# k of batch 0's second and last third on 96 and 112 partitions, where it was on 94 and 100, in a windowed-attention and ReGLU kernel

## The chip, the cores and the metric

The kernel runs on one core of a Trainium2 chip. The core has five engines with a program each: TensorE (PE, matmuls; its weight loads are shown apart as PEld), VectorE (DVE), ScalarE (ACT), GpSimd (POOL) and SyncE (SP, which here only issues transfers). They work in parallel, each in the order of its own program, and wait for each other by semaphores. 16 DMA engines move data between the memory of the device and SBUF, the core's memory of 128 partitions. The metric is the device time of one execution in microseconds (us), the median of three runs; lower is better. The profile is of one further execution, and its span is a little shorter than the device time.

## The reference

Attention for 4 batches of 8 heads, 768 positions and head size 64, in which a query sees the first 4 positions ("sinks") and the last 128; then a ReGLU feed-forward (FFN) over all 3072 tokens.

```python
scores = scale * np.matmul(q, k.transpose(0, 1, 3, 2))
keep = is_sink | in_window          # pos < 4, or 0 <= i - j < 128
scores = np.where(keep, scores, -1000000000.0)
scores = scores - np.max(scores, axis=-1, keepdims=True)
a = np.exp(scores)
a = a / (np.sum(a, axis=-1, keepdims=True) + 1e-09)
attn = np.matmul(a, v)
x = attn.transpose(0, 2, 1, 3).reshape(3072, 512)
out = (np.maximum(x @ w_gate, 0) * (x @ w_val)) @ w_out   # d_ff 1536
```

All inputs and the output are float32.

## The kernel before

**Units.** The attention is cut into units of one head pair (two heads, 128 rows of head dimension together). The first batch is cut into thirds along the positions, so that the FFN can begin after a third: kinds A (positions 0 to 251), B (252 to 499) and C (500 to 767), four units each (A0 to A3, B0 to B3, C0 to C3), in this order. Batches 1 to 3 have four units each of kind F (all 768 positions). The table `GEO` (line 22) holds each kind's geometry. Its entry `k=(r0, pp, nn)` says how k is loaded: from row r0 on, on pp partitions with nn consecutive rows each, pp times nn rows in all. B and C need some rows ahead of their first query, for the window: B the keys 124 to 499, C 372 to 767.

**Steps of a unit.** `load_kq` (line 136) issues two transfers for k, one for each head, then two for q; a partition's nn rows are contiguous in device memory, 1 KB for nn = 4. They land in float32 staging tiles: `kf`, `qf` for A, C and F, and for B in `stage`, which borrows the memory of a later tile (line 435). `cast` (line 157) makes bfloat16 of them on POOL (`kn`, `qn`, `vn`). `T` (line 178) transposes k and q on PE, nn transposes for k, and copies them out of PSUM: ACT writes `kT` (line 191), DVE and ACT one half of `qz` each (line 200), and for each key block that has the sinks ACT a copy of 124 of its columns into `kTs` (line 213). `S` (line 226) is scores, exp on ACT (line 236) and mask on DVE (line 238). `V` (line 240) multiplies by v, in which a block of ones also gives the row sums; `norm0` (line 368) divides on DVE and writes `xT`, the input of the FFN, for batch 0 without a way through memory.

Which rows of k stand in which transpose follows from pp and nn, and so do the column of `kTs`' source, `p0 = (124 * j + 4 - self.kr) // kn_` (line 212), and the size of the copy at line 191. Nothing else in the code knows the partition count.

**FFN.** `chunk(b, c0, n, m)` (line 387) does one block of 128 hidden columns of n tokens: four matmuls with `wg` (line 392), relu on ACT, four with `wv` (line 398), product on DVE. `ffn2` (line 404) does the second matmul with `wo` (line 411) and stores the result. Chunks of 0 to 11 belong to A's tokens, 12 to 23 to B's, and so on. A chunk of the first block waits for `xT` of all four A units. `load_w(c)` loads columns for chunks 3c to 3c+2 of each block, with a conversion to bfloat16 during the transfer; it is issued from POOL.

**Order.** All is written out by hand in program order; there is no planner. SP's queue first issues A's loads, then those of the four B units, for each k, q and v (lines 436 to 438), then C's; a load for a later unit waits until the buffer it writes is free. The A units are done one after the other, with the casts and transposes of B0 and B1 between them. Weight loads are calls in this order too: `load_w(0)` behind the casts of A2, `load_w(1)` behind the casts of B0, `load_w(2)` behind those of B1, `load_w(3)` behind those of k and q of B2. Since POOL issues them in its own program order, a cast that waits for its data holds back the weight load behind it.

Then stages of attention (`unit_stages`, line 500) are put between the chunks by the function `want` (line 557): chunk ci is preceded by so many stages, in the first block 1.5 on average, and a B unit has three: S; T of the next unit with the casts of the one after it; V of the unit before it. The transposes of B1 stand ahead of chunk 0, those of B2 ahead of chunk 2, those of B3 ahead of chunk 4, in PE's program.

Of the kernel before, what the change touches and what calls it, by code (L numbers as in the profile page):

```python
# [21 lines left out]
GEO = {  # L22
    "A": dict(q0=0, n=252, q=(0, 128, 2), k=(0, 128, 2), js=(0, 1), sink=(1,),
              groups=[[(0, 0, 255), (1, 128, 128)]], parts=[(0, 256, [(0, 0, 255), (1, 128, 128)])]),
    "B": dict(q0=252, n=248, q=(252, 128, 2), k=(124, 94, 4), js=(1, 2, 3), sink=(2,),
              groups=[[(1, 252, 127), (2, 252, 248), (3, 376, 132)]],
              parts=[(252, 256, [(1, 252, 127), (2, 252, 248), (3, 376, 132)])]),
    "C": dict(q0=500, n=268, q=(480, 96, 3), k=(368, 100, 4), js=(3, 4, 5, 6), sink=(4, 6),
              groups=[[(3, 480, 147), (4, 500, 248)], [(5, 624, 144), (6, 748, 20)]],
              parts=[(480, 288, [(3, 480, 147), (4, 500, 248), (5, 624, 144), (6, 748, 20)])]),  # L30
    "F": dict(q0=0, n=768, q=(0, 128, 6), k=(0, 128, 6), js=(0, 1, 2, 3, 4, 5, 6), sink=(1, 3, 5),
# [589 lines left out]
```

The softmax here doesn't subtract the row's maximum and nothing guards it: scores larger than these inputs give would overflow.

## Time and profile before

| what | value |
|---|---|
| device time, median of 3 | 329.45 us (328.45 to 330.43) |
| span of the profiled execution | 326.9 us |
| PE busy | 263.6 us (81%), 1868 matmuls |
| DVE, ACT, POOL busy | 164.7, 163.4, 95.4 us |
| chain that ended last | PE 52% of the span |
| DMA | 33.64 MB, mean 103 GB/s |
| loads of k for B | 8 issues of 94 KB, from SP |
| loads of k for C | 8 issues of 100 KB, from SP |

Busy shares are means over the span; the page's second part cuts the span into 40 slices of 8.2 us, one digit each, in tenths. A row of the timeline has start, duration, engine, line, operation, output <- input, shape and count, and in brackets the idle time ahead of it on its engine, with what ended that. "SPq" is SP's queue: the duration is that of issuing, not of the transfer. The list of waits has the sum in us, how often, and the longest. In a table of windows each engine has its busy time and its count of instructions; the last three columns are the granted PE clock (1.00 is full), the busy share of the 16 DMA engines (it can pass 1 where packets of two queues overlap on an engine) and the rate in GB/s.

### The profile page before, as it was taken

To read this page: it belongs to the slowest core of one execution; us is meant where nothing else is said; L and a number is where in the kernel's file an instruction comes from. 1 tells how busy PE (TensorE), PEld (TensorE's weight loads), DVE (VectorE), ACT (ScalarE), POOL (GpSimd) and SP (SyncE) were. 2 spreads that over 40 slices of the span, in tenths; PEclk is the share of its full clock that TensorE was granted. 3 is DMA by queue.
4 is the path that set the end of the run, shared out by engine and by line. 5 is a ranking of instruction groups with operands and counts; after the bars stand their busy time and mean duration, and the time that the engine had idled before them with its cause. 6 is when DMAs were issued, how large, how long until landed. Compare 5 with 4: busy or idle time off the path is not lost.

```text
span 326.9 us, 5251 instructions
## 1 busy us (share of the span) xinstructions
PE 263.6 (81%) x1868; PEld 171.3 (52%) x1868; DVE 164.7 (50%) x340; ACT 163.4 (50%) x300; POOL 95.4 (29%) x159
## 2 busy tenths in 40 slices
PE   2443355665668888775999999999999999999995
PEld 1222244553447776553666666666666555555552
DVE  4467141764777557754364746565553542332220
ACT  5643233564457887453556566565764333333321
POOL 7626215454456555705040505042000000000000
PEclk9999875987989999999899999999999999999999
DMA  4769894948569868839192845253422120111002
GB/s 130 123 122 170 126 167 118 191 87 146 117 131 109 162 106 141 173 84 170 53 185 73 166 115 91 81 61 88 55 66 65 36 80 35 41 50 40 32 32 96
DMA packets 55313, 33.64 MB, mean 103 GB/s; under 512 B 34268, under 2 KB 51436, under 8 KB 55288
## 3 DMA queue, kind: packets, MB, share of 16 engines
q1 hardware_dynamic: 25096, 25.48, 27.1%
q0 software_dynamic: 29104, 7.57, 24.0%
q10 hardware_dynamic: 1088, 0.26, 0.4%
q8 instruction: 14, 0.23, 0.3%
q14 instruction: 11, 0.09, 0.1%
HBM read 34.43 MB, written 6.44 MB: 125 GB/s over the span
## 4 chain that ended last, share of the span: by engine, by line
PE 52%; ACT 0%; issue 0%; ACTq 0%
PE op L411 17%; PE vp L398 14%; PE gp L392 14%; PE ops L248 3%; PE sps L232 2%; PE tq L195 1%; PE tk L188 1%; ACT ot L415 0%; ACTq L415 0%
## 5 line engine op out<-in xcount | busy, mean ns | idle before, releaser
L400 DVE TENSOR_TENSOR hT<-gs,vp 128x384 bf16<-128x384 f32 (+3 forms) x108 | 54.6, 506 | 73.0 <-PE vp L398 59.4
L398 PE MATMUL vp<-xT,wv 128*128 128x384 bf16 (+3 forms) x432 | 83.6, 318 | 4.0 <-ACT gs L395 2.1
L392 PE MATMUL gp<-xT,wg 128*128 128x384 bf16 (+3 forms) x432 | 83.8, 318 | 3.8 <-DVE xT L364 3.8
L411 PE MATMUL op<-wo,hT 128*128 128x512 bf16 x288 | 79.0, 383 | 0.0
L395 ACT ACTIVATE gs<-gp 128x384 f32<-128x384 f32 (+3 forms) x108 | 49.2, 456 | 40.3 <-PE gp L392 39.6
L398 PEld LDWEIGHTS <-wv 128*128 128x128 bf16 x432 | 43.7, 101 | 30.1 <-issue 8.5
L236 ACT ACTIVATE ee<-sps 128x1006 bf16<-128x1006 f32 (+6 forms) x52 | 47.1, 906 | 15.9 <-PE sps L232 15.4
L238 DVE TENSOR_TENSOR ee<-ee,msk 128x1006 bf16<-128x1006 bf16 (+6 forms) x52 | 37.2, 715 | 33.5 <-ACT ee L236 33.5
L392 PEld LDWEIGHTS <-wg 128*128 128x128 bf16 x432 | 40.8, 101 | 19.4 <-issue 0.2
L151 POOL DMA_DIRECT2D vn<-in_v_dram x32 | 26.2, 824 | 73.6 <-PE ops L248 69.5
L411 PEld LDWEIGHTS <-hT 128*128 128x128 bf16 x288 | 28.4, 99 | 23.0 <-issue 0.6
L188 PE MATMUL tk<-ident,kn 128*128 128x128 bf16 (+2 forms) x112 | 11.7, 244 | 33.7 <-POOL kn L163 33.2
L248 PE MATMUL ops<-ee,vn 128*128 128x248 bf16 (+9 forms) x264 | 29.1, 253 | 8.9 <-ACT qz L200 5.1
L232 PE MATMUL sps<-qz,kT 128*128 128x251 bf16 (+6 forms) x136 | 28.8, 266 | 5.2 <-ACT kT L191 1.9
L248 PEld LDWEIGHTS <-vn 128*128 128x128 bf16 x264 | 23.4, 105 | 18.0 <-issue 8.7
L191 ACT COPY kT<-tk 128x768 bf16<-128x768 bf16 (+3 forms) x24 | 14.9, 622 | 32.5 <-PE tk L188 32.4
L364 DVE TENSOR_TENSOR xT<-oab,R 64x768 bf16<-64x768 f32 x24 | 24.2, 1007 | 10.1 <-DMA R<-rcp_tmp 10.0
L252 ACT COPY oab<-ops 65x752 f32<-65x752 f32 (+1 forms) x24 | 19.1, 795 | 20.1 <-PE ops L248 20.0
L188 PEld LDWEIGHTS <-kn 128*128 128x128 bf16 (+2 forms) x112 | 8.4, 110 | 39.5 <-POOL kn L163 36.2
L200 DVE COPY qz<-tq 64x768 bf16<-64x768 bf16 (+2 forms) x24 | 16.5, 686 | 20.9 <-PE tq L195 20.8
L232 PE MATMUL sps<-qz,kTs 128*128 128x248 bf16 (+3 forms) x104 | 25.9, 272 | 0.0
L200 ACT COPY qz<-tq 64x768 bf16<-64x768 bf16 (+2 forms) x24 | 14.1, 585 | 22.9 <-DVE qz L200 21.6
(61 smaller groups left out, 188.6 us busy)
## 6 DMA issues: line engine op xcount, KB each, us to landing
out_dram<-ot SPq DMA_DIRECT2D x24, 256.0 KB
kf<-in_k_dram SPq DMA_DIRECT2D x24, 192.0 KB
qf<-in_q_dram SPq DMA_DIRECT2D x24, 192.0 KB
R<-rcp_tmp SPq DMA_DIRECT2D x12, 384.0 KB
vn<-in_v_dram POOLq DMA_DIRECT2D x24, 96.0 KB, 3.4
wg<-in_moe_w_gate_dram POOLq DMA_DIRECT2D x4, 384.0 KB, 8.6
wv<-in_moe_w_val_dram POOLq DMA_DIRECT2D x4, 384.0 KB, 11.4
wo<-in_moe_w_out_dram POOLq DMA_DIRECT2D x3, 512.0 KB, 7.9
```

Of the source, the lines that this page charges most:

```text
L151: eng.dma_start(out=dst[:, o + j0:o + j0 + nj, h, 0:64], in_=bass.AP(src.tensor, src.offset + 124 * j0 * D, [[D, 128], [124 * D, nj], [1, ...
L200: (nc.scalar.copy if h else nc.vector.tensor_copy)(qz[s][r, h, z0:z0 + qp * qn_].rearrange("d (p n) -> d p n", n=qn_), pq[r, 0:qp * qn_].r ...
L232: nc.tensor.matmul(out=ps[:, h, c:c + w], lhsT=self.kw(j), rhs=qz[s][:, h, self.zo + qa:self.zo + qa + w], start=True, stop=True)
L236: nc.scalar.activation(x, ps[:, :, 0:c], Act.Exp, bias=0.0, scale=scale)
L238: nc.vector.tensor_tensor(x, x, bc(msk[:, m0:m0 + c], 2), op=Alu.mult)
L248: nc.tensor.matmul(out=ps[:, h, qa - q0:qa - q0 + w], lhsT=vn[s][:, self.vo + j, h, :], rhs=ee[s][:, gi, h, c:c + w], start=i == 0, stop=i ...
L364: nc.vector.tensor_tensor(xTs[b][64 * h:64 * h + 64, p, :], oab[0:64, h, :], R[:, h, :], op=Alu.mult)
L392: nc.tensor.matmul(out=gp[:, 0:n], lhsT=wg[:, ko, m * 128:(m + 1) * 128], rhs=x[:, ko, c0:c0 + n], start=ko == 0, stop=ko == KO - 1)
L395: nc.scalar.activation(gs[:, 0:n], gp[:, 0:n], Act.Relu, bias=0.0, scale=1.0)
L398: nc.tensor.matmul(out=vp[:, 0:n], lhsT=wv[:, ko, m * 128:(m + 1) * 128], rhs=x[:, ko, c0:c0 + n], start=ko == 0, stop=ko == KO - 1)
L400: nc.vector.tensor_tensor(hT[:, m, c0:c0 + n], gs[:, 0:n], vp[:, 0:n], op=Alu.mult)
L411: nc.tensor.matmul(out=op, lhsT=hTs[b][:, m, t * 128:(t + 1) * 128], rhs=wo[:, m, :], start=m == 0, stop=m == FM - 1)
```

## The change

Two entries of the table change. B's k is loaded from row 116 on 96 partitions with 4 rows each (384 rows, up to row 499 as before), where it was row 124 on 94 partitions (376 rows); C's from row 320 on 112 partitions (448 rows), where it was row 368 on 100 (400 rows). The eight and 48 rows more lie ahead of what is needed, and are read and transposed for nothing. It is for the way in which a transfer is spread over the DMA engines, which goes by the number of partitions.

```diff
-    "B": dict(q0=252, n=248, q=(252, 128, 2), k=(124, 94, 4), js=(1, 2, 3), sink=(2,),
+    "B": dict(q0=252, n=248, q=(252, 128, 2), k=(116, 96, 4), js=(1, 2, 3), sink=(2,),
...
-    "C": dict(q0=500, n=268, q=(480, 96, 3), k=(368, 100, 4), js=(3, 4, 5, 6), sink=(4, 6),
+    "C": dict(q0=500, n=268, q=(480, 96, 3), k=(320, 112, 4), js=(3, 4, 5, 6), sink=(4, 6),
```

No instruction is added, removed or moved on any engine. For eight units the transposes of k get 96 and 112 columns for 94 and 100, ACT's copies at line 191 384 and 448 columns for 376 and 400, POOL's casts of k two and twelve partitions more, and the transfers are wider accordingly. The start columns of the `kTs` copies move with r0, and their widths stay.

## The prediction

> **What bounds the kernel now.** I began with the page's 40 slices (8.2 us each): where is TensorE (PE) not full?
>
> ```profile
> PE   2443355665668888775999999999999999999995
> DMA  4769894948569868839192845253422120111002
> ```
>
> Full from slice 20 on: whatever is saved ahead of that only counts if the late part starts earlier. The first seven slices (to 57 us) are at 20 to 50%. So next the waits, with the window 14 to 54 us:
>
> ```profile
> POOL kn L163 <- DMA stage<-in_k_dram: 22.1, 4, 8.6
> PEld L188 <- POOL kn L163: 18.8, 4, 6.3
> PE tk L188 <- POOL kn L163: 17.5, 4, 6.1
> ACT kT L191 <- PE tk L188: 17.0, 4, 6.2
> ```
>
> This is one chain, seen on four engines: GpSimd (POOL) waits four times, 22.1 us in all, for k of the second third (kind B); its cast frees PE's transposes, these ScalarE's (ACT) copy. Nothing overtakes: PE runs in program order, the FFN chunks behind the transposes. The timeline of POOL gives the dates:
>
> ```profile
> 20.07 0.61 POOL L163 CAST kn<-stage 94x512 bf16<-94x512 f32 x1 [5.76 <-DMA stage<-in_k_dram]
> 28.54 2.23 POOL L163 CAST kn<-stage 94x512 bf16<-94x512 f32 x1 [2.44 <-DMA stage<-in_k_dram]
> 38.65 0.61 POOL L163 CAST kn<-stage 94x512 bf16<-94x512 f32 x1 [5.30 <-DMA stage<-in_k_dram]
> 50.81 0.61 POOL L163 CAST kn<-stage 94x512 bf16<-94x512 f32 x1 [8.59 <-DMA stage<-in_k_dram]
> ```
>
> and that of PE what stands behind them (chunks 0, 2 and 4 are the L392 rows that follow each transpose):
>
> ```profile
> 30.83 0.49 PE L188 MATMUL tk<-ident,kn 94*128 94x94 bf16 x4 [4.42 <-POOL kn L163]
> 31.36 1.05 PE L392 MATMUL gp<-xT,wg 128*128 128x252 bf16 x4
> ...
> 39.32 0.50 PE L188 MATMUL tk<-ident,kn 94*128 94x94 bf16 x4 [4.24 <-POOL kn L163]
> ...
> 51.48 0.50 PE L188 MATMUL tk<-ident,kn 94*128 94x94 bf16 x4 [6.06 <-POOL kn L163]
> ...
> 53.03 1.05 PE L392 MATMUL gp<-xT,wg 128*128 128x252 bf16 x4
> ```
>
> Why is k late? Is the DMA full? Two windows, one while only B's loads run (weights landed), one under a weight load; the last columns are granted clock, DMA share, GB/s:
>
> ```profile
> 20.00:23.00 3.00, 1.42 (x11) 1.10 (x12) 1.58 (x4) 0.47 (x1) 1.00 (x2) 1.00 0.17 27
> 15.00:19.00 4.00, 1.53 (x9) 0.88 (x7) 3.25 (x8) 2.93 (x6) 0.00 (x0) 1.00 1.26 216
> ```
>
> POOL waits through both. In the first the 16 engines are busy to 0.17, which is 2.7 engines, and move 27 GB/s; in the second 216 GB/s, 13.5 per engine. 27/13.5 = 2 engines. B's loads crawl over about two engines while fourteen lie idle. The issuing queue feels it too: two k loads take 0.72 us to issue at 10.7 us, but
>
> ```profile
> 31.95 5.06 SPq L142 DMA_DIRECT2D stage<-in_k_dram  x2
> 37.05 5.83 SPq L142 DMA_DIRECT2D stage<-in_q_dram  x2
> ```
>
> **What the skill says.** (1) The Trainium skill, "DMA: Bandwidth & Descriptors", section "Why a DMA increments its semaphore by 16 and not by 1": a DMA runs on the largest k up to 16 that divides the slowest dimension of both sides; it names 128 or 96 partitions as 16 and 100 as 10. By that rule 94 = 2 x 47 gives 2, 112 gives 16. The trace agrees for 94 (2.0 engines above); for 100 it shows nothing separately. (2) Same page, "Issuing engines are not separate DMA queues": loads from SyncE and from GpSimd share the same 16 engines. The trace agrees: k lands slowest where weights run beside it (8.6 us of waiting). (3) "TensorE: Matmul & The Clock Gate", Part 1: an idle stretch of about 3.4 us halves PE's clock. Agrees: 0.50 granted at 39 to 42 us, after the gap from 35.1 to 39.3.
>
> **The change, part by part.**
>
> *B's k on 16 engines.* A pair of k loads (two heads, 94 rows of 1 KB each) puts 94 KB on each of two engines; now 192 rows on 16, 12 KB each. Engine 0 also carries 8 KB of q and 12 KB of v per unit (128-partition tiles, evenly shared), so per unit 114 KB become 32, for four units 456 become 128 KB. At the 13.5 GB/s of a loaded engine: 34 us become 9.5. The old span, first issue 10.7 to last cast 50.8, is 40 us, so this accounts for it. k, q, v of each unit queue in this order, so q and v come early too.
>
> *What then holds the first third.* I walk the old timelines without the k waits. B0's k would be there at about 14.5, when POOL has done A's last piece (14.3). T of B0 then follows S of A3 on PE at 17.9 and not 20.7. VectorE (DVE) is the next limit: its mask of A3 ends at 21.1 in any case; then qz, which came at 22.50, at 21.1, so ACT's qz, kTs and output copies are 1.4 us earlier. DVE's chain of two normalisations, 24.33 to 28.42, starts at 22.9 and ends at 27.0. That gives xT of A3, for which chunk 0 waits; T of B1 no longer does (needed at 24.6, k there by 18 to 20). Chunk 0: 27.0, not 31.36. Saved 4.4.
>
> *Chunks 0 to 4.* Unhindered pace: chunk 4 starts at 53.03, chunk 9 at 66.47 (same timeline), 13.44/5 = 2.7 us, with transposes, scores, sums and copies of one unit per two chunks included. Chunk 4 thus starts at 27.0 + 4 x 2.7 = 37.8, not 53.03: 15.2 saved.
>
> *Do the weights hold it up?* POOL issues them between the casts: now at 10.7, 24.6, 31.9, 40.7. Without k waits at about 11, 17, 20.5, 24. One pair is 0.79 MB as written; four, with four B units (2.1 MB), make 5.2 MB, at 215 GB/s 24 us: all landed at about 36 to 38. Chunk 3 (36) needs the second pair, chunk 6 (43) the third, chunk 9 (51) the fourth. Hidden, with little to spare; B3's k is wanted at 37 too.
>
> *After 54 us.* I take the rest to move as a block: POOL's waits there are for PE and for its own v loads, the units go one by one, and PE is full from 150 us on.
>
> *Added work.* Wider transposes (280 ns for 94x94 and 227 for 100x100 in different clocks, so width is lost in them); ACT's kT copies: 472 ns for 376 columns, 492 for 400, 0.8 ns a column: 4 x 8 + 4 x 48 columns = 0.2 us, at most. More bytes: 4 x 4 + 4 x 24 KB = 112 KB, 0.5 us of the full DMA, spread. Casts have the same length per partition (610 and 604 ns for 94 and 100): nothing. All of it lies beside the new slack.
>
> *C's k on 16 engines.* 100 KB on ten engines becomes 112 on 16. Only one wait of 0.7 us is put down to it: at most 0.7, which I leave out, since C's loads are issued early.
>
> Sum: 329.45 - 15.2 = **314.2 us**. Unknown costs: landing under a saturated DMA (k for B3 0 to 3 us late), pace (1.8 to 2.9 us between single chunks in the trace, 2.2 to 2.9 as a mean): saving 12 to 17.
>
> **Rivals.**
> 1. *DMA as a whole takes over.* All weights now go out within 15 us on top of B's loads. For: under the first weight load the mean over 10 to 20 us is only 149 GB/s. 5.2 MB at 149 GB/s is 35 us, so B3's k might land at 45.6 and its transpose start at 46.3, not 51.5: 5 saved; half-way cases 7 to 10. Against: order of need agrees with order of issue, and the full windows do 211 to 222 GB/s. About 322 us.
> 2. *More than the sum.* With no gap over 3.4 us PE keeps its clock (0.59 at 50 to 60 us before), and the pace becomes 2.2: chunk 4 at 35.8, 17.2 saved, and a share of the 0.91 clock at 57 to 120 us (9% of 45 us busy = 4, half on the path): about 310.
> 3. *No change*, 329: the wait is total contention and the spread gives nothing. Against: 27 GB/s and 0.17.
> 4. *Slower than before.* The saving dies in a later wait, while denser traffic makes each of the v loads, 4.6 us to land in the median between 55 and 120 us, about 1 us longer; four of them for C are waited for one by one: 333. For it: POOL idles 22.2 us for these landings. Against: first 15 us would have to vanish, and no row after 54 us is tied to a date.
>
> **How the numbers follow.** Forecast (12 to 17 saved) 0.72; rival 1 0.14; rival 2 0.08; rivals 3 and 4 0.03 each. Range 308 to 322: above it rivals 3, 4 and part of 1. Faster 0.94, same 0.03, slower 0.03.
>
> **What would show it.** Right: the four waits of the kn cast for the B loads nearly gone (under 5 us in all), issue of k and q pairs back near 1 us, the second to fourth weight issues before 27 us, chunk 0 at 27, chunk 4 at 36 to 40, the stretch behind it as long as before. Step "chunk 0" is wrong if xT of A3 does not come at 27; step "weights" if PE waits in chunks 3 to 9 for a weight DMA, or B's casts still wait with a DMA share above 1; the block assumption, if chunk 4 is early and full PE is not. The prediction fails outright if 96 partitions still move 27 GB/s.

## The result, and the profile after

| | before | after |
|---|---|---|
| device time, median | 329.54 us (328.45 to 330.43) | 313.94 us (312.14 to 314.40) |
| ratio to before | | 0.9518, 95% interval 0.9470 to 0.9566 |
| span of the profiled execution | 326.9 us | 310.4 us |

15.6 us less (4.8%); 314.2 was forecast, in a range from 308 to 322. The profiled execution of the changed kernel is the fastest of its four (312.14 us), so dates read from the two profiles differ by about a microsecond more than the medians do.

The slices of the page after (each is now 7.8 us):

```profile
PE   1545856466798997749999999999999999999995
DMA  5799997855898778391919373524312301000002
```

The DMA is now busy to 0.9 or more from the third slice to the sixth, and PE's thin stretch is shorter. In the list of waits the first line of the chain that opened the prediction is 2.8 us where it was 22.1, and PE's transposes of B no longer wait for the cast:

```profile
POOL kn L163 <- DMA stage<-in_k_dram: 2.8, 2, 1.6
```

The four casts of B's k on GpSimd's timeline were at 20.1, 28.5, 38.7 and 50.8 us:

```profile
15.89 0.60 POOL L163 CAST kn<-stage 96x512 bf16<-96x512 f32 x1 [1.58 <-DMA stage<-in_k_dram]
...
22.57 0.63 POOL L163 CAST kn<-stage 96x512 bf16<-96x512 f32 x1
...
25.75 0.63 POOL L163 CAST kn<-stage 96x512 bf16<-96x512 f32 x1
...
29.38 0.61 POOL L163 CAST kn<-stage 96x512 bf16<-96x512 f32 x1 [1.25 <-DMA stage<-in_k_dram]
```

On PE's timeline chunk 0, the transposes of B3 and chunk 4 were at 31.4, 51.5 and 53.0 us:

```profile
26.54 1.05 PE L392 MATMUL gp<-xT,wg 128*128 128x252 bf16 x4
...
37.10 0.33 PE L188 MATMUL tk<-ident,kn 96*128 96x96 bf16 x4 [0.57 <-ACT ee L236]
37.39 0.59 PE L392 MATMUL gp<-xT,wg 128*128 128x252 bf16 x4
```

B3's transposes now wait for a PSUM buffer that ScalarE's exp frees, not for k: its k was cast seven us earlier. The prediction would have failed outright if 96 partitions still moved 27 GB/s. In the window in which it read 27 GB/s and a share of 0.17, the changed kernel has (the last columns are PE clock, DMA share, GB/s):

```profile
20.00:23.00 3.00, 0.80 (x4) 0.36 (x3) 2.18 (x5) 1.39 (x5) 2.85 (x5) 1.00 0.96 204
```

Longer windows of the changed kernel show the price:

```profile
14.00:50.00 36.00, 22.39 (x180) 16.89 (x178) 26.78 (x74) 20.38 (x48) 17.45 (x33) 1.00 1.20 215
50.00:52.00 2.00, 1.00 (x14) 0.95 (x14) 0.97 (x4) 1.37 (x5) 1.38 (x4) 1.00 0.00 0
```

For 36 us the DMA moves 215 GB/s, as much as in the full windows of the prediction, and at 50 us the backlog is gone. The kernel before, from 14 to 54 us:

```profile
14.00:54.00 40.00, 16.78 (x109) 11.96 (x107) 18.60 (x56) 13.90 (x32) 12.53 (x22) 0.84 0.80 143
```

How much earlier is each chunk than before? That is read from the L392 rows of both timelines, in pairs:

| chunk | 0 | 4 | 8 | 12 | 16 | 20 | 33 | 38 and all later ones to 61 |
|---|---|---|---|---|---|---|---|---|
| earlier by, us | 4.8 | 15.6 | 14.8 | 17.4 | 17.0 | 17.0 | 18.2 | 16.5 |

### The profile page after: what moved, and what is told of

It is laid out like the page before. It is cut to its first block, busy times and chain, and to the rows that moved or that the text cites. A ratio compares the mean times of both kernels' runs of the same rounds, so it can differ in the third digit from the quotient of the medians.

```text
span 310.4 us, 5251 instructions
## 1 busy us (share of the span) xinstructions
PE 259.5 (84%) x1868; PEld 168.2 (54%) x1868; DVE 167.5 (54%) x340; ACT 163.2 (53%) x300; POOL 93.7 (30%) x159
## 4 chain that ended last, share of the span: by engine, by line
PE 55%; ACT 0%; issue 0%; ACTq 0%
PE op L411 18%; PE vp L398 15%; PE gp L392 15%; PE ops L248 3%; PE sps L232 3%; PE tk L188 1%; PE tq L195 1%; ACT ot L415 0%; ACTq L415 0%
## 5 line engine op out<-in xcount | busy, mean ns | idle before, releaser
L392 PE MATMUL gp<-xT,wg 128*128 128x384 bf16 (+3 forms) x432 | 82.6, 315 | 4.5 <-DVE xT L364 4.5
L398 PE MATMUL vp<-xT,wv 128*128 128x384 bf16 (+3 forms) x432 | 82.7, 315 | 2.9 <-ACT gs L395 2.1
L238 DVE TENSOR_TENSOR ee<-ee,msk 128x1006 bf16<-128x1006 bf16 (+6 forms) x52 | 38.6, 742 | 32.5 <-ACT ee L236 32.4
L236 ACT ACTIVATE ee<-sps 128x1006 bf16<-128x1006 f32 (+6 forms) x52 | 47.1, 906 | 14.7 <-PE sps L232 14.3
L392 PEld LDWEIGHTS <-wg 128*128 128x128 bf16 x432 | 40.1, 100 | 18.9
L248 PE MATMUL ops<-ee,vn 128*128 128x248 bf16 (+9 forms) x264 | 28.2, 246 | 13.5 <-ACT qz L200 7.5
L248 PEld LDWEIGHTS <-vn 128*128 128x128 bf16 x264 | 22.6, 101 | 23.0 <-issue 13.8
L232 PE MATMUL sps<-qz,kT 128*128 128x251 bf16 (+6 forms) x136 | 27.5, 258 | 7.6 <-ACT qz L200 2.4
L252 ACT COPY oab<-ops 65x752 f32<-65x752 f32 (+1 forms) x24 | 19.0, 794 | 21.1 <-PE ops L248 21.0
L364 DVE TENSOR_TENSOR xT<-oab,R 64x768 bf16<-64x768 f32 x24 | 23.9, 996 | 11.2 <-DMA R<-rcp_tmp 10.9
L232 PE MATMUL sps<-qz,kTs 128*128 128x248 bf16 (+3 forms) x104 | 25.0, 263 | 0.0
L415 ACT COPY ot<-op 128x512 f32<-128x512 f32 x24 | 14.0, 584 | 18.3 <-PE op L411 18.3
L191 ACT COPY kT<-tk 128x768 bf16<-128x768 bf16 (+3 forms) x24 | 15.1, 629 | 15.5 <-PE tk L188 15.4
```

The lines of the kernel that those rows point to most:

```text
L232: nc.tensor.matmul(out=ps[:, h, c:c + w], lhsT=self.kw(j), rhs=qz[s][:, h, self.zo + qa:self.zo + qa + w], start=True, stop=True)
L236: nc.scalar.activation(x, ps[:, :, 0:c], Act.Exp, bias=0.0, scale=scale)
L238: nc.vector.tensor_tensor(x, x, bc(msk[:, m0:m0 + c], 2), op=Alu.mult)
L248: nc.tensor.matmul(out=ps[:, h, qa - q0:qa - q0 + w], lhsT=vn[s][:, self.vo + j, h, :], rhs=ee[s][:, gi, h, c:c + w], start=i == 0, stop=i ...
L364: nc.vector.tensor_tensor(xTs[b][64 * h:64 * h + 64, p, :], oab[0:64, h, :], R[:, h, :], op=Alu.mult)
L392: nc.tensor.matmul(out=gp[:, 0:n], lhsT=wg[:, ko, m * 128:(m + 1) * 128], rhs=x[:, ko, c0:c0 + n], start=ko == 0, stop=ko == KO - 1)
```

## The experiments

Ratios are to the kernel before, run on the same chip. Dates are of one profiled execution for each kernel, and such dates vary: in the seven kernels here that load B's k on 96 partitions, the cast of B3's k began between 29.4 and 32.4 us. So a difference of one to three us between two profiles is only a hint, unless the times show it as well.

**One half of the change at a time.** `b_only` and `c_only`:

```diff
-    "B": ... k=(124, 94, 4)        # b_only: this line alone
+    "B": ... k=(116, 96, 4)
...
-    "C": ... k=(368, 100, 4)       # c_only: this line alone
+    "C": ... k=(320, 112, 4)
```

> B's k on 96 partitions, C's left at 100. Theory (the two k loads of a B unit sat on two DMA engines; B's loads alone held the first third): nearly all of the gain, ratio to before 0.950 to 0.957 (313 to 315.5 us). Rival (C's spread from ten to 16 engines is what shortened the stretch behind chunk 9, by 2.6 us up to chunk 12): 316 to 317 us, chunk 12 no more than 15 us earlier than before.

> C's k on 112 partitions, B's left at 94. Theory: no change that can be told, ratio 0.995 to 1.003, since only 0.7 us of waiting was put down to C's k. Rival (C's part is worth 2 to 3 us): ratio 0.99 to 0.993. In both the four waits for B's k stay at 20 to 23 us.

`b_only`: 313.95 us, 0.9539 (0.9494 to 0.9585), the gain of the whole change. `c_only`: 326.55 us, 0.9949 (0.9926 to 0.9973): some gain, of 0.5%, between what the two theories gave. The four waits for B's k stay in `c_only`, their sum to the tenth:

```profile
POOL kn L163 <- DMA stage<-in_k_dram: 22.1, 4, 8.6
```

The rival of `b_only` was right in one point: its chunk 12 is 14.0 us earlier than before, in the full change 17.4. GpSimd waits 4.1 us for C0's k there and 1.5 in the changed kernel, but this isn't where the 3.4 us arise: chunks 4 to 9 are 0.6 to 1.0 us earlier in `b_only`, and C0's v is issued at 45.6 where it is 46.4. It lands later, and so does C1's. GpSimd's timeline in `b_only`, where the changed kernel has waits of 2.1 and 5.8 us:

```profile
53.27 0.39 POOL L176 COPY vn<-vsink 4x256 bf16<-4x256 bf16 x1 [5.51 <-DMA vn<-in_v_dram]
...
64.09 0.39 POOL L176 COPY vn<-vsink 4x256 bf16<-4x256 bf16 x1 [6.59 <-DMA vn<-in_v_dram]
```

Half of the 3.4 us is given back later (14.8 against 16.5 us from chunk 38 on). Whether C's spread or the variation between executions makes v late is not shown, and the times of the two kernels can't be told apart. So B's 96 partitions are the change; C's 112 are worth between nothing and 1.7 us.

**The same 94 rows on more engines.** `b_split` takes the kernel before and cuts each k load of B in two:

```diff
                 for h in range(2):
-                    eng.dma_start(out=dst[0:pp, h, :], ...)
+                    for a, z in ((0, 80), (80, 94)) if pp == 94 else ((0, pp),):
+                        eng.dma_start(out=dst[a:z, h, :], ...)
```

> Before, with each k load of B cut in two, 80 and 14 partitions: the same 94 rows and the same bytes on the same partitions, 16 more issues on SyncE of about 0.45 us each, C as before. Theory (the count of partitions sets how many engines carry a load, and nothing else of the change matters): 313 to 317 us, waits for k under 5 us. Rival (the gain comes from the number of partitions itself or the alignment of the rows, not from the spread): 327 to 330 us; the extra issues would make it slower still.

315.68 us, 0.9602 (0.9544 to 0.9659). Partitions, rows, bytes and casts are those of before; only the shape of a transfer differs (80 is 5 x 16, and 14 its own divisor), and SyncE issues 16 more. So it isn't the 96 partitions or the first row as such. The waits for k are 7.1 us and not under 5; the last one, on GpSimd's timeline:

```profile
34.76 0.61 POOL L164 CAST kn<-stage 94x512 bf16<-94x512 f32 x1 [3.54 <-DMA stage<-in_k_dram]
```

This is 2.4 us later than in `b_only`, with 12 KB of each pair on the fullest engine in both. B3's k was issued 0.9 us later (24.5 against 23.6); the rest is open.

**Wider, but on few engines.** `b_122` and `b_116` take the changed kernel with other counts for B:

```diff
-    "B": ... k=(116, 96, 4)
+    "B": ... k=(12, 122, 4)        # b_122: 122 = 2 x 61
...
+    "B": ... k=(36, 116, 4)        # b_116: 116 = 4 x 29
```

> The changed kernel with B's k on 122 partitions (from row 12), 122 = 2 x 61. By the skill's rule two engines carry each load: 122 + 20 KB per unit on engine 0, 568 KB for the four units, at 13.5 GB/s 42 us where 94 partitions took 34. Theory: slower than before by 5 to 9 us, 334 to 339 us, SyncE's issues of 3 us and more. Rival (wider is better, or more than 94 is enough): 314 to 318 us.

> The changed kernel with B's k on 116 partitions (from row 36), 116 = 4 x 29, four engines: engine 0 carries 58 + 20 = 78 KB per unit where it was 114 and is 32. Theory (a threshold: k is only worth the wait until VectorE's chain is the later one; B3's k at about 33 us, wanted at 37): within 1.5 us of the changed kernel, ratio to before 0.95 to 0.96. Rival (the gain goes in proportion to the bytes on the fullest engine): 36/82 of the gain, some 7 us, ratio 0.977 to 0.982.

`b_122`: 331.72 us, 1.0104 (1.0064 to 1.0144), 1% slower than before, with more partitions than either kernel. The cast of B3's k on GpSimd's timeline, and an issue on SyncE's:

```profile
57.02 0.61 POOL L163 CAST kn<-stage 122x512 bf16<-122x512 f32 x1 [10.89 <-DMA stage<-in_k_dram]
```

```profile
16.59 6.82 SPq L142 DMA_DIRECT2D stage<-in_k_dram  x2
```

The direction is as expected and the size is not: chunk 4 is 5.2 us later than before, and from chunk 38 on 2.3. C's 112 partitions may give 1.3 of this back (so much in `c_only`'s profile); where the other 1.6 went is open.

`b_116`: 321.43 us, 0.9777 (0.9729 to 0.9824). Here my expectation fell: I had B3's k at 33 us, and it came at 41.5, after PE was ready for it. GpSimd's timeline, then PE's:

```profile
41.52 0.62 POOL L163 CAST kn<-stage 116x512 bf16<-116x512 f32 x1 [8.67 <-DMA stage<-in_k_dram]
```

```profile
42.19 0.57 PE L188 MATMUL tk<-ident,kn 116*128 116x116 bf16 x4 [6.11 <-POOL kn L163]
```

The time is the rival's, but the dates speak against proportion: k is again late for its use. I had counted B's bytes alone on the fullest engine; the weights, 49 KB of each pair on every engine if they are evenly spread, run on it too. With them:

| B's k on | KB of B up to B3's k on the fullest engine | and four weight pairs | first issue to B3's cast | KB per us |
|---|---|---|---|---|
| 94 partitions, 2 engines | 3 x 114 + 94 = 436 | 632 | 50.8 - 10.7 = 40.1 us | 15.8 |
| 122 partitions, 2 engines | 3 x 142 + 122 = 548 | 744 | 57.0 - 10.7 = 46.3 us | 16.1 |
| 116 partitions, 4 engines | 3 x 78 + 58 = 292 | 488 | 41.5 - 10.6 = 30.9 us | 15.8 |

About one rate explains the three, with the engine counts of the rule in the Trainium skill, "DMA: Bandwidth & Descriptors", section "Why a DMA increments its semaphore by 16 and not by 1" (the largest divisor up to 16). Without the weights the three would be 10.9, 11.8 and 9.4 KB per us. It is an estimate, and the weights are counted high: half of the fourth pair before (up to 24 KB) and all of it in `b_116` (49 KB) landed only behind B3's cast, which leaves 15.2 and 14.2 KB per us at the least.

With 16 engines B3's k comes at 29.4 us, ahead of its use at 37.1, and the wait is gone. That is the threshold: 116 partitions miss it by 5 us (their transposes start at 42.2). `b_split` is on its other side: its k came 5.4 us later than in the changed kernel, and chunk 4 is 15.5 us earlier than before, where the changed kernel has 15.6.

**Is the full DMA a bound now?** `extra_load` adds to the changed kernel a pair of weight transfers that nothing reads:

```diff
     def load_w(c):
         n = d_ff // 4
+        if c == 1:
+            for i, w in enumerate((moe_w_gate, moe_w_val)):
+                nc.gpsimd.dma_start(out=spare[:, i, :, :], in_=...[:, :, 0:n])
```

> The changed kernel with one more pair of weight transfers (0.79 MB as written, into a spare tile that nothing reads), issued just ahead of the second pair. It adds 3.7 us of the full DMA at 215 GB/s, and 1.5 us of issuing on GpSimd. Theory (the DMA is full from 14 to 45 us but not on the path): chunk 4 within 1 us of the changed kernel's 37.4, time within 1.5 us of it. Rival (DMA as a whole has become the bound): 3 to 4 us slower than the changed kernel, chunk 4 at 40 to 41.

319.09 us, 0.9698 (0.9659 to 0.9737), 5 to 6 us slower than the changed kernel. My theory was right on chunk 4 (38.4, 1.0 us later) and wrong on the time. The loss lies behind it: chunk 9 is 1.2 us later, chunk 12 6.5. There GpSimd waits for the v loads of C0 and C1, which it issues behind the weights and w_out; its timeline, and the row of PE that waits for the cast behind the second:

```profile
55.65 0.40 POOL L177 COPY vn<-vsink 4x256 bf16<-4x256 bf16 x1 [6.41 <-DMA vn<-in_v_dram]
...
67.21 0.39 POOL L177 COPY vn<-vsink 4x256 bf16<-4x256 bf16 x1 [7.30 <-DMA vn<-in_v_dram]
```

```profile
68.21 0.55 PE L189 MATMUL tk<-ident,kn 112*128 112x112 bf16 x4 [7.28 <-POOL kn L164]
```

In the changed kernel the same waits, on GpSimd's timeline, are 2.1 and 5.8 us:

```profile
50.62 0.39 POOL L176 COPY vn<-vsink 4x256 bf16<-4x256 bf16 x1 [2.10 <-DMA vn<-in_v_dram]
...
60.68 0.39 POOL L176 COPY vn<-vsink 4x256 bf16<-4x256 bf16 x1 [5.83 <-DMA vn<-in_v_dram]
```

C0's v is issued 0.7 us later than in the changed kernel (47.1 against 46.4), and the copy that waits for it begins 5.0 us later. So the backlog that ends at 50 us is not a bound of B's chunks, but C's first v load stands at its end.

**What holds the first third.** `masks_early` moves `setup_m1()`, 1.4 us of VectorE, to an idle stretch ahead:

```diff
                 A[p + 2].T(*GV)
+                if p == 0:
+                    setup_m1()
...
         V0(NP - 1)
-        setup_m1()
```

> The changed kernel with setup_m1 (12 mask instructions on VectorE, 1.4 us, between the last normalisation of A and the first mask product of B) moved ahead to where VectorE waits, behind the transposes of A2 at 11.5 us. Theory (VectorE's chain now holds the first third): scores of B1 at 28.8 instead of 30.1, all behind them 1.0 to 1.4 us earlier, ratio to before 0.945 to 0.952. Rival (transfers hold it): no change against the changed kernel.

312.83 us, 0.9507 (0.9476 to 0.9539): against 0.9518 for the changed kernel nothing that can be told. In the profile chunk 0 is 0.6 us later, chunks 1 to 6 are 0.8 to 1.5 us earlier, which fits the theory (VectorE's chain holds this part), and chunk 12 is 1.6 us later: v of C1 on GpSimd's timeline is waited for longer, 6.6 against 5.8 us.

```profile
62.31 0.39 POOL L176 COPY vn<-vsink 4x256 bf16<-4x256 bf16 x1 [6.56 <-DMA vn<-in_v_dram]
```

`masks_wo` also issues the third load of w_out right behind the second:

```diff
-                if 2 <= x < 5:
-                    load_wo(x - 2)
+                if x == 2:
+                    load_wo(0)
+                if x == 3:
+                    load_wo(1)
+                    load_wo(2)
```

> masks_early, and the third load of w_out issued right behind the second (0.5 MB, at about 43 us), not at 52 us ahead of the v loads of C1, which then take 5.8 us to be waited for. Theory (units of C go at the pace of their v loads): v of C1 2 us earlier, chunk 12 at 59 to 60; a part of it is given back up to chunk 37, so 0.5 to 1.5 us less than masks_early. Rival (the load delays v of C0 instead): no change or up to 1 us more than masks_early.

313.06 us, 0.9507 (0.9475 to 0.9540): the rival. v of C1 is waited for 3.9 us, but v of C0, now behind two loads of w_out, for 7.1.

**w_out behind v.** In all kernels so far w_out goes out ahead of C's v loads. `wo_late` (on the changed kernel), `wo_late_masks` (with `masks_early`) and `before_wo_late` (on the kernel before) turn this round:

```diff
                             nxt.load_v(nc.gpsimd, False)
+                            if 3 <= x < 6:
+                                load_wo(x - 3)
...
-                if 2 <= x < 5:
-                    load_wo(x - 2)
```

> The changed kernel with the three loads of w_out (0.5 MB each as written) issued on GpSimd right behind the v loads of C0, C1 and C2, not ahead of them; chunks 12, 16 and 20, which need them first, start at 62, 79 and 89 us. Theory (after the change the DMA's backlog, full from 14 to 49.7 us, reaches C's v loads, which stand in line behind w_out): v of C0 and C1 waited for 0 to 2 and 3 to 5 us where it was 2.1 and 5.8; chunk 12 at 58 to 61; 1 to 3 us less than the changed kernel, ratio to before 0.943 to 0.95. Rival (what delays v is the k and q of later units from the other queue, or the v load itself): no change within 0.5 us.

> wo_late and masks_early together. Theory: the 0.9 to 1.2 us that masks_early had up to chunk 6 and lost at C's v loads are kept now: 0.5 to 1.2 us less than wo_late, ratio to before 0.939 to 0.947. Rival (the slack goes elsewhere): as wo_late.

> The kernel before with w_out's loads behind C's v loads as in wo_late. There the DMA had time: v of C0 and C1 were waited for 4.9 and 5.6 us, the second and third load of w_out issued 3.4 and 0.8 us ahead of them. If w_out ahead of v is what counts, 1 to 3 us less than before (ratio 0.99 to 0.997); if only the backlog that the change brought counts, no change.

`wo_late`: 310.00 us, 0.9416 (0.9381 to 0.9450). GpSimd's timeline in it, with the two waits that were 2.1 and 5.8 us:

```profile
51.30 0.39 POOL L176 COPY vn<-vsink 4x256 bf16<-4x256 bf16 x1 [1.05 <-DMA vn<-in_v_dram]
...
59.99 0.39 POOL L176 COPY vn<-vsink 4x256 bf16<-4x256 bf16 x1 [4.43 <-DMA vn<-in_v_dram]
```

`wo_late_masks`: 308.74 us, 0.9365 (0.9323 to 0.9406), the fastest kernel of the study; that the masks add to `wo_late` is not settled, as the intervals meet. `before_wo_late`: 324.11 us, 0.9830 (0.9783 to 0.9877), 5.1 us less, which is more than I expected. The order mattered before the change too: its chunk 9 starts when it did before (66.5), and chunk 12 is 4.7 us earlier. Whether v waited there for w_out in the queue of GpSimd or on the engines is not separated; the same two waits in it, and then in the kernel before:

```profile
64.97 0.39 POOL L176 COPY vn<-vsink 4x256 bf16<-4x256 bf16 x1 [0.76 <-DMA vn<-in_v_dram]
...
73.33 0.39 POOL L176 COPY vn<-vsink 4x256 bf16<-4x256 bf16 x1 [3.84 <-DMA vn<-in_v_dram]
```

```profile
68.21 0.39 POOL L176 COPY vn<-vsink 4x256 bf16<-4x256 bf16 x1 [4.85 <-DMA vn<-in_v_dram]
...
78.06 0.39 POOL L176 COPY vn<-vsink 4x256 bf16<-4x256 bf16 x1 [5.60 <-DMA vn<-in_v_dram]
```

## Why the prediction was right, step by step

*Two engines.* Right. `b_split` gets most of the gain with 94 rows, and `b_122` loses it with 122; the four waits fell from 22.1 to 2.8 us. But the window from which the count came was misread, and that 27/13.5 gave 2 was in part luck. It was taken for one in which the weights had landed and only B's loads ran. The DMA queues in it, 20 to 23 us of before (packets, MB, share of 16 engines):

```profile
q0 software_dynamic: 68, 0.05, 10.5%
q1 hardware_dynamic: 117, 0.03, 6.4%
```

The first is GpSimd's queue, the weights, and holds 1.7 engines' time; the second is SyncE's, with B's loads. So the end of a weight pair was still running beside k while most engines lay idle; on which engines, the view doesn't say.

*The size of B's loads, "34 us become 9.5".* The mechanism was right and the term was too small: it left out the weights, which share the engine. That the old span came to 40 us should have said so, and so should the window above; I took the first as agreement. For the forecast it did no harm, since with 16 engines k is early in either count; it misled the expectation for `b_116` by 8.5 us.

*Chunk 0 at 27.0.* It came at 26.5. B0's k was cast at 15.9 and not 14.5 (at 14.3 to 16.8 in the other kernels with 96 partitions), and VectorE's chain hid this: its qz copy, forecast for 21.1, began at 21.04, and xT of A3, which only the last of the chunk's first four matmuls needs, was ready at 27.1.

*Pace 2.7 us, chunk 4 at 37.8.* It came at 37.4; (37.39 - 26.54)/4 = 2.7. This agreement is in part luck: the steps were uneven (4.6, 2.2, 2.2, 1.9), the first because S of B1 waits for copies that stand behind VectorE's masks, and the others near the 2.2 of rival 2. With the masks moved (`masks_early`) the mean is 2.3. The clock kept, as rival 2 had it (1.00 from 14 to 50 us, where it was 0.84 up to 54), but no gain of it is seen behind chunk 4: chunks 4 to 9 took 14.2 us, and 13.4 before.

*Weights.* Issued at 10.7, 21.1, 24.3 and 26.7, not at 11, 17, 20.5 and 24, because casts ahead of them waited for B0's q and v. The last landed at 42.4, not at 36 to 38. No chunk waited for a weight; chunk 9, the first to need the last pair, began at 51.6. "Hidden, with little to spare" holds for chunks 0 to 9 only. I hadn't asked what GpSimd issues behind the weights: C's v loads. Rival 4 had named these loads, but in the changed kernel's profile the four of C are waited for 15.3 us, where it was 17.6. Rival 1 (the DMA takes over) was nearer than its chance of 0.14 says, in another place than I had put it: 0.79 MB more, as in `extra_load`, and 5 to 6 us of the gain are gone.

*The rest moves as a block.* Right on the whole: 15.6 us earlier at chunk 4 and 16.5 from chunk 38 on, with 14.8 to 18.2 between, in a profile that is the fastest of its four. That the medians differ by the 15.6 us of chunk 4 is chance.

*C's k, "left out".* `c_only` gives 0.5% alone, beside B's change nothing can be told: mis-sized by 0 to 1.7 us.

*Added work.* Hidden as forecast: ScalarE's copies took 477 ns for 384 columns and 531 for 448.

## What to carry to other kernels

In these kernels the partition count of a transfer decided how many DMA engines carried it. Look for a low DMA share beside a wait for a DMA, ask which queues make up that share, and try a count that is a multiple of 16 (or cut the transfer), even if rows are then read for nothing. Count on the fullest engine all that runs on it, weights included, and compare the landing with the date at which the data is wanted: a spread pays up to that date and no further. When transfers become faster, see what is issued behind them: here small loads that a later stage waited for gained by going ahead of big ones that were wanted late.

## What I had not expected

A narrow transfer holds back the queue that issues it: a pair of B's k loads took 0.8 to 1.4 us to issue in the changed kernel, with the DMA full, but up to 5.1 us before and 6.8 us in `b_122`, where two engines carry it. So what stands behind it in the queue was held up too: B3's q, on 128 partitions, began to issue 5.1 us behind its k before, and 1.5 in the changed kernel. And the order of w_out and v alone was worth 5.1 us in the kernel before and, by the ratios, some 3.4 in the changed one, with 1.5 MB of w_out among 33.6 MB in all.
